# Inverting the first four chunks' triangles by 16 x 16 blocks, with the block products one chunk at a time

## The chip, the cores and the metric

The kernel runs on one core of a Trainium2 chip. Times are device microseconds (us) of one execution. The kernel before took 814.61, 817.60 and 818.12 us in three runs, a median of 817.6 us. One further execution was profiled and took 815.66 us. The engines are named as in the profile: PE (TensorE matmul, with PEld its weight load), DVE (VectorE), ACT (ScalarE), POOL (GpSimd) and SP (SyncE, which here only issues transfers).

## The reference

An attention block with a recurrent state is followed by a feed-forward block. With B = 4 batches, H = 8 heads, S = 768 steps and head size D = 40 the reference computes

```python
for t in range(S):
    y[:, :, t] = einsum('bhd,bhde->bhe', rt, state)
    Sa = einsum('bhde,bhe->bhd', state, at)
    state_decay = state * wt[:, :, None, :] - einsum('bhd,bhe->bhde', Sa, bt)
    state = state_decay + einsum('bhd,bhe->bhde', vt, kt)
x = y.transpose(0, 2, 1, 3).reshape(B * S, H * D)      # 3072 tokens of 320
h = x @ w_in                                           # 320 x 2048
out = (h * cos(h)) @ w_out                             # 2048 x 320
```

All inputs are float32 except that the two weight matrices arrive as float64, seen by the kernel as pairs of 32-bit words.

## The kernel before

**Chunks.** The 768 steps are cut into 24 chunks of C = 32, so that batch x step fills 128 partitions. Within a chunk the recurrence becomes a triangular system of 32 x 32 for each batch and head. Four chunks at a time share one inversion: 4 chunks x 4 batches x 8 heads = 128 triangles, held as the tile `inv` with one triangle part on each partition.

**Preparation of a group of chunks** (`p1_w`, `p1_a`, `p1_b`, `p1_n`): decays `w`, vectors `a` and `b` are loaded, transposed by PE and scaled; `p1_n` multiplies them into the triangles `nps`, which ACT copies to `nt`. `inv_start` (L465) transposes `nt` into `u` on DVE.

**Two ways to invert.** `inverse` (L547) runs `inv_step` (L472) for j = 31 down to 1, each one DVE multiply (L476) and one DVE subtract (L480), then one transpose into `rt` (L484). It serves chunks 0 to 3 and 8 to 23. `by_blocks` (L541) serves chunks 4 to 7 alone. It inverts the two diagonal 16 x 16 blocks together in 15 pairs (`pair_step`, L502 and L507), turns the first block into `rn` (`pair_turn`, L513), and leaves the lower left block to PE: `pair_first` multiplies the raw triangle `noff` by `rn` and ACT copies the product to `half` (L523); `pair_second` multiplies that by the second block and DVE adds the product into `rt` (L535). For this `p1_n` also copies the triangles to `noff` (L455), for chunks 4 to 7 only.

**Work of a chunk c.** `p2_in` and `p2_kn` put v, r and k into padded tiles on POOL; `p2_v`, `p2_k`, `p2_g` transpose them and form two Gram matrices (`gram`, then `ag` and `vvm`). The chain through the state `qz` is `ch_t` (transposes `sT`), `ch_q` (`qps`), `ch_x` (`x0ps`, copied to `x`), `ch_s` (`sps`: `x` times the inverse `rt`, copied to `sm`) and `ch_z` (`dps`; DVE and POOL update `qz` at L721 and L722, and `yt` goes through memory into the token tile `xT`). Chunk 0 starts from a zero state and has no `ch_t` and no `ch_q`.

**The feed-forward block** is cut into pieces: `first_a` and `first_b` (matmuls `ph`, then the cosine on ACT and DVE) and `second` (matmuls `po`). Pieces fill places marked `M` in each chunk's list from chunk 2 on. The weights must be turned into float32 beforehand. `rounded` makes this from 20 tiles of 512 columns: a transfer of `words`, four DVE operations (L241, L242, L251, L257), three on ACT (L245, L247, L254) and one on POOL (L260). These steps wait in the list `w_steps`; `step` takes some after each piece of chunk work (`fill` gives how many).

**Order.** Everything is written out by hand: each engine runs its instructions in the order in which the Python code emits them. `step` also counts down `later` entries, which is how loads and stores get their place in SP's queue. `busy` and `kept_busy` put idle matmuls on PE, `shifted` puts tiny ones. In the built program every transfer from SP waits for the completion of the one eight issues before it. `load` (L146) issues four transfers of 40 KB for one input of one chunk. The tiles `nat_k`, `nat_v` and `nat_r` exist once: their next load waits for POOL to have read them.

**Start of the program** (L953 to L979): preparation of chunks 0 to 3, the decay scan of `w` for chunks 4 to 7 (`scanned(1)`, stored to memory as `wd`), then the 31 inverse steps with the `p2` work of chunks 0 and 1 and `ch_x` of chunk 0 between them.

## Time and profile before

| | before |
|---|---|
| median of three runs | 817.6 us (814.61 to 818.12) |
| profiled execution | 815.66 us |
| its span, first to last instruction | 813.8 us |
| PE busy | 752.8 us, 93% of the span |
| DVE busy | 498.2 us, 61% |
| ACT busy | 385.2 us, 47% |
| POOL busy | 201.3 us, 25% |
| mean granted PE clock | 0.968 of full speed |
| PE busy, 0 to 100 us | 60.2 us |
| PE busy, 100 to 200 us | 93.1 us |
| PE busy, 300 to 700 us | 397.1 us of 400 |

The span is what the engines' records cover; the profiled time has 1.9 us more around it. A group of instructions is shown as line, engine, operation, result <- operands, shapes and count. "Idle before <- X" says what ended the wait ahead of an instruction; "issue" is a wait for nothing that the profile shows. SPq is SP's queue: the time of issuing a transfer, not of moving it. The page cuts the span into 40 slices of 20.3 us, with the busy share in tenths.

### The profile page before, as it was taken

Reading aid. Unit: us, or ns where it says so; the run is one execution under the profiler, and the core shown is the slowest. Engines: PE = TensorE matmul, PEld = TensorE weight load, DVE = VectorE, ACT = ScalarE, POOL = GpSimd, SP = SyncE. Lnnn points to the kernel's source line nnn. Section 1 sums busy time; section 2 is a strip of 40 time slices with the busy share of each in tenths; the row PEclk is TensorE's granted clock in tenths of the full one; section 3 lists DMA queues with packets and bytes.
Section 4 is the critical chain, followed back from the end, with each engine's and each line's share of the span. In section 5 each row is a group of like instructions: output and inputs, shape, how many; then the busy total and the mean of one; then the engine's idle time right before and its main releaser. Section 6 shows DMA issues by size and latency. Waiting matters only on the chain.

```text
span 813.8 us, 38932 instructions
## 1 busy us (share of the span) xinstructions
PE 752.8 (93%) x17472; PEld 579.2 (71%) x17472; DVE 498.2 (61%) x1052; ACT 385.2 (47%) x713; POOL 201.3 (25%) x353
## 2 busy tenths in 40 slices
PE   3647899899899999999999999999999999999997
PEld 3533568677678777777777777777777777777775
DVE  6987888865555797454796554894346773332231
ACT  1214777554255446446436535534635445364352
POOL 5314454430213221231330330331130222201000
PEclk9856899999999999999999999999999999999999
DMA  7366654354144324333214314213220212101000
GB/s 122 59 153 156 188 135 132 52 123 68 44 96 96 62 37 75 69 88 68 62 37 70 100 32 66 60 40 69 50 45 21 45 37 56 24 14 36 19 17 16
DMA packets 183301, 55.74 MB, mean 68 GB/s; under 512 B 157152, under 2 KB 178656, under 8 KB 183136
## 3 DMA queue, kind: packets, MB, share of 16 engines
q1 hardware_dynamic: 180560, 51.95, 29.7%
q8 instruction: 137, 2.24, 1.2%
q10 hardware_dynamic: 2320, 0.98, 0.6%
q0 software_dynamic: 256, 0.33, 0.2%
q14 instruction: 28, 0.23, 0.1%
HBM read 42.07 MB, written 11.14 MB: 65 GB/s over the span
## 4 chain that ended last, share of the span: by engine, by line
PE 67%; DVE 16%; ACT 5%; issue 4%; SPq 4%; DMA 3%; POOL 1%; DVEq 0%; ACTq 0%; POOLq 0%
PE ph L101 22%; PE po L101 20%; SPq L152 4%; PE x0ps L101 4%; PE dps L101 3%; DVE inv_tmp L476 3%; DVE inv L480 3%; PE gram L101 3%; PE vT L326 3%; DVE rw L391 2%; PE sps L101 2%; PE nps L101 2%; PE qps L101 2%; PE sT L623 1%; PE busy L101 1%
## 5 line engine op out<-in xcount | busy, mean ns | idle before, releaser
L101 PE MATMUL po<-w_out_sb,gT 128*128 128x320 f32 x768 | 224.7, 441 | 0.0
L101 PE MATMUL ph<-xT,w_in_sb 128*128 128x256 f32 x768 | 185.3, 386 | 0.6 <-issue 0.6
L101 PEld LDWEIGHTS po<-w_out_sb,gT 128*128 128x128 f32 x768 | 140.8, 191 | 54.7 <-issue 2.5
L101 PEld LDWEIGHTS ph<-xT,w_in_sb 128*128 128x128 f32 x768 | 139.2, 190 | 29.6 <-issue 12.2
L795 ACT ACTIVATE turns<-ph,rnd 128x512 f32<-128x512 f32 x96 | 64.2, 686 | 155.3 <-PE ph L101 154.9
L797 DVE SCALAR_TENSOR_TENSOR turns<-turns,ph 128x512 f32<-128x512 f32 x96 | 64.1, 684 | 116.1 <-ACT turns L795 115.8
L805 DVE TENSOR_TENSOR gT<-ph,turns 128x512 f32<-128x512 f32 x96 | 65.7, 686 | 36.0 <-ACT turns L802 36.0
L722 POOL TENSOR_TENSOR qz<-qz,wc 128x160 f32<-128x160 f32 x92 | 43.0, 486 | 152.1 <-DVE qz L721 151.1
L802 ACT ACTIVATE turns<-turns,half_pi 128x512 f32<-128x512 f32 x96 | 69.3, 722 | 3.1
L801 ACT ACTIVATE turns<-turns 128x512 f32<-128x512 f32 x96 | 60.1, 626 | 18.9 <-DVE turns L797 18.9
L480 DVE TENSOR_TENSOR inv<-inv,inv_tmp 128x31 f32<-128x31 f32 (+15 forms) x155 | 61.9, 399 | 5.3
L476 DVE TENSOR_TENSOR inv_tmp<-u,inv 128x31 f32<-128x31 f32 (+15 forms) x155 | 59.3, 382 | 3.5
L555 POOL COPY vp<-nat_v 128x320 f32<-128x320 f32 x25 | 12.2, 489 | 183.2 <-DMA nat_v<-in_v_dram 113.6
L101 PE MATMUL ph<-xT,w_in_tail 64*128 64x256 f32 x384 | 54.5, 402 | 0.0
L721 DVE TENSOR_TENSOR qz<-dps,qz 128x160 f32<-128x160 f32 x92 | 29.0, 315 | 33.6 <-PE dps L101 33.5
L391 DVE RECIPROCAL rw<-nat_w 128x320 f32<-128x320 f32 x20 | 42.8, 2142 | 0.0
L627 ACT COPY s<-sT 128x512 f32<-128x512 f32 x46 | 24.5, 584 | 37.5 <-PE sT L623 37.5
L101 PEld LDWEIGHTS <-idle 32*64 32x64 bf16 (+2 forms) x566 | 24.7, 95 | 22.2 <-issue 17.1
L101 PEld LDWEIGHTS ph<-xT,w_in_tail 64*128 64x128 f32 x384 | 33.0, 186 | 9.1 <-issue 5.3
L733 POOL TENSOR_TENSOR yt<-yt,wb 128x512 f32<-128x512 f32 x24 | 31.6, 1316 | 22.1 <-DVE yt L728 22.1
L611 ACT COPY vvm<-gram 128x256 f32<-128x256 f32 x24 | 8.8, 367 | 55.4 <-DVE ag L606 55.0
L392 POOL TENSOR_TENSOR bn<-nat_b,rw 128x320 f32<-128x320 f32 x22 | 19.6, 890 | 57.5 <-DVE rw L391 46.1
(131 smaller groups left out, 1106.0 us busy)
## 6 DMA issues: line engine op xcount, KB each, us to landing
words<-in_moe_w_in_dram SPq DMA_DIRECT2D x8, 512.0 KB
nat_k<-in_k_dram SPq DMA_DIRECT2D x96, 40.0 KB
nat_v<-in_v_dram SPq DMA_DIRECT2D x96, 40.0 KB
nat_r<-in_r_dram SPq DMA_DIRECT2D x96, 40.0 KB
xd<-yt SPq DMA_DIRECT2D x48, 80.0 KB
out_dram<-ot SPq DMA_DIRECT2D x24, 160.0 KB
nat_b<-in_b_dram SPq DMA_DIRECT2D x88, 40.0 KB
wd<-ws SPq DMA_DIRECT2D x5, 640.0 KB
```

Source lines behind the costliest of these rows:

```text
L101: nc.tensor.matmul(o, lhsT=lhsT, rhs=rhs, start=start, stop=stop, skip_group_check=True)
L152: via.dma_start(nat[n, c][blk[i], :, :D], at_c.rearrange("h t d -> t h d"))
L391: nc.vector.reciprocal(rw, wn)
L476: nc.vector.tensor_tensor(tmp, u[:, j : j + 1, :j].to_broadcast([P, C - j, j]), x[:, j:, j : j + 1].to_broadcast([P, C - j, j]), ALU.mult,)
L480: nc.vector.tensor_tensor(x[:, j:, :j], x[:, j:, :j], tmp, ALU.subtract)
L722: nc.gpsimd.tensor_tensor(z, z, wc.rearrange("p (f m b) -> p f m b", f=2, m=2)[:, :, :, bb] .unsqueeze(3).to_broadcast([P, 2, 2, D]), ALU. ...
L733: nc.gpsimd.tensor_tensor(yt.rearrange("p j b t -> p (j b) t"), yt.rearrange("p j b t -> p (j b) t"), wx, ALU.mult)
L795: nc.scalar.activation(n, u, ACTF.Identity, bias=rnd, scale=1.0)
L797: nc.vector.scalar_tensor_tensor(n, n, -ROUND, u, ALU.add, ALU.subtract)
L801: nc.scalar.activation(n, n, ACTF.Abs)
L802: nc.scalar.activation(n, n, ACTF.Sin, bias=half_pi, scale=-2.0 * math.pi)
L805: nc.vector.tensor_tensor(gT[:, 2 * e : 2 * e + 2].rearrange("p f t -> p (f t)"), us[e], ns[e], ALU.mult)
```

## The change

`by_blocks` now also makes the inverse of chunks 0 to 3, so `noff` is copied for them too. Their block products are emitted one chunk at a time, ahead of that chunk's `ch_s`: `pair_first(0, 0)` and `pair_second(0, 0)` at the start, F1 and S1 in chunk 1, F2, S2, F3 and S3 in chunk 2. For chunks 0 to 3 `rn` lies in `bn_b[6]` and `half` in `bn_b[4]` and `bn_b[5]`, which are not used for chunks 4 to 6 until later. The products of chunks 4 to 7 become four and four (F4 to F7, S4 to S7) in place of one and three. Loads of `a` and `b` for chunk 4 and `a` for chunk 5 go right behind chunk 0's k, v, r; two weight tiles are fetched next, ahead of chunk 1's k, v, r; `w` of chunks 4 and 5 and `b` of chunk 5 move from the start into chunk 1. The idle matmuls are put in other places and numbers, and `shifted` is 0 at the start where it was 111.

```diff
     bn_b = kept("bn", [P, H, DP], 7, 0.0, padding)
+    for i in (4, 5):
+        nc.gpsimd.memset(bn_b[i][:, :, C // 2 : C], 0.0)
     kn_b = kept("kn", [P, H, DP], 2, 0.0, padding)
...
             G["nt"] = sb1.tile([P, C, 4, 2, HH], F32, tag="nt", name="nt")
-            if c == 4:
+            if c < 8:
                 G["noff"] = sb2.tile([P, 4, 2, HH, C], F32, tag="rt", name="noff")
...
             )
-        if 4 <= c < 8:
+        if c < 8:
             for e in range(2):
...
 
-    def pair_turn():
-        G["rn"] = sb1.tile([P, 4 * H, HB], F32, tag="nt", name="rn")
-        G["half"] = sb1.tile([P, 4 * H, C], F32, tag="u", name="half")
-        nc.gpsimd.memset(G["half"][:, :, HB:], 0.0)
+    def pair_turn(c):
+        if c:
+            G["rn"] = sb1.tile([P, 4 * H, HB], F32, tag="nt", name="rn")
+            G["half"] = sb1.tile([P, 4 * H, C], F32, tag="u", name="half")
+            nc.gpsimd.memset(G["half"][:, :, HB:], 0.0)
+        else:
+            G["rn"] = bn_b[6].rearrange("p h d -> p (h d)").rearrange("p (n u) -> p n u", u=HB)
         nc.vector.transpose(
...
 
-    def pair_first(lo, hi):
-        ps = at("below")[:, 0]
+    def pair_space(c, done, pool, tag):
+        if c or done:
+            return at("below")[:, 0]
+        return pool.tile([P, 512], F32, tag=tag, name="below")
+
+    def pair_half(c, i):
+        return G["half"][:, H * i : H * (i + 1)] if c else bn_b[4 + i % 2][:, :, :C]
+
+    def pair_first(c, i, moe=True):
+        ps = pair_space(c, moe, ps_h, "h")
         nt = G["noff"].rearrange("p c e j t -> p (c e j) t")
-        for n in range(H * lo, H * hi):
+        half = pair_half(c, i)
+        for n in range(H):
             for g in range(B):
-                mm(ps[blk[g], HB * n : HB * (n + 1)], nt[blk[g], n, :], G["rn"][blk[g], n, :], n == H * lo)
-        nc.scalar.copy(
-            G["half"][:, H * lo : H * hi, :HB],
-            ps[:, H * lo * HB : H * hi * HB].rearrange("p (n u) -> p n u", u=HB),
-        )
-
-    def pair_second(c, lo, hi):
-        ps = at("below")[:, 0]
-        rt = G["rts"].rearrange("p c h t -> p (c h) t")
-        for n in range(H * lo, H * hi):
+                mm(
+                    ps[blk[g], HB * n : HB * (n + 1)], nt[blk[g], H * i + n, :],
+                    G["rn"][blk[g], H * i + n, :], n == 0,
+                )
+        nc.scalar.copy(half[:, :, :HB], ps[:, : H * HB].rearrange("p (n u) -> p n u", u=HB))
+        if c + i == 3:
+            nc.gpsimd.memset(padding(bn_b[6]), 0.0)
+
+    def pair_second(c, i, moe=True):
+        ps = pair_space(c, moe, ps_o, "o")
+        half, rt = pair_half(c, i), G["rts"][:, i]
+        for n in range(H):
             for g in range(B):
-                mm(ps[blk[g], HB * n : HB * (n + 1)], G["half"][blk[g], n, :], rt[blk[g], n, HB:], n == H * lo)
-        to = rt[:, H * lo : H * hi, HB:]
+                mm(ps[blk[g], HB * n : HB * (n + 1)], half[blk[g], n, :], rt[blk[g], n, HB:], n == 0)
+        to = rt[:, :, HB:]
         nc.vector.tensor_tensor(
-            to, to, ps[:, H * lo * HB : H * hi * HB].rearrange("p (n u) -> p n u", u=HB), ALU.add
-        )
-        for i in range(lo, hi):
-            G["rt", c + i] = G["rts"][:, i]
+            to, to, ps[:, : H * HB].rearrange("p (n u) -> p n u", u=HB), ALU.add
+        )
+        G["rt", c + i] = rt
 
...
             inv_start, *(lambda j=j: pair_step(j) for j in range(HB - 1, 0, -1)),
-            pair_turn, lambda: inv_end(c, True),
+            lambda: pair_turn(c), lambda: inv_end(c, True),
         ]
...
                     later(1, lambda i=i: load(6 + i, "ab"))
-            elif c >= 2 and c + 3 < NCH:
+            elif c > 4 and c + 3 < NCH:
                 for m in range(6):
-                    later(
-                        8 + m // 3 if c == 2 else (9 if c == 6 else 2) + m, lambda m=m: load(c + 2 + m % 2, "wab"[m // 2])
-                    )
+                    later((9 if c == 6 else 2) + m, lambda m=m: load(c + 2 + m % 2, "wab"[m // 2]))
 
...
         first, other = p1(0), p1(2)
-        for seg in (*first[:2], *other[:2], *first[2:], *other[2:]):
+        for seg in first[:2]:
             step(seg)
+        load(4, "ab")
+        load(5, "a")
+        for seg in (*other[:2], *first[2:], *other[2:]):
+            step(seg)
+        for m in range(2):
+            w_work[m][0]()
         scanned(1)
...
         p2_kn(0)
-        inv_steps.extend(inverse(0))
+        inv_steps.extend(by_blocks(0))
         v, k, g = p2(0)
         v1, k1, g1 = p2(1)
-        for n, seg in ((12, v), (0, k), (0, g), (6, main(0)[2]), (6, None), (4, v1), (0, k1), (0, g1)):
+        x0, s0, z0 = main(0)[2:]
+        for n, seg, idle_n in ((6, v, 0), (0, k, 0), (0, g, 4), (4, x0, 6), (2, v1, 5)):
             for _ in range(n):
                 inv_steps.pop(0)()
-            if seg:
-                step(seg)
-            else:
-                for m in range(3):
-                    w_work[m][0]()
-                p2_in(1)
+            step(seg)
+            if seg is x0:
+                w_work[2][0]()
                 p2_kn(1)
-        N_PAD = {0: 111, 19: 75}
-        shifted(N_PAD[0])
-        while inv_steps:
+            busy(idle_n)
+        while len(inv_steps) > 2:
             inv_steps.pop(0)()
-            if 2 < len(inv_steps) < 9:
-                busy(1, True)
+        step(k1)
+        busy(2)
+        all_of(inv_steps)
+        step(g1)
+        busy(3)
+        N_PAD = {0: 0, 19: 75}
+        step(lambda: pair_first(0, 0, False))
         for m in range(3, 5):
             w_work[m][0]()
+        step(lambda: pair_second(0, 0, False), 0, 1)
+        step(s0, 0, 3)
+        busy(6)
+        step(z0, 0, 4)
+        busy(4)
+        for n, c, name in ((3, 4, "w"), (5, 5, "w"), (7, 5, "b")):
+            later(n, lambda c=c, name=name: load(c, name))
 
...
         M = object()
-        FILL = {(1, 4): 12, (1, 7): 16, (2, 0): 10, (2, 2): 14, (2, 3): 6, (2, 8): 37, (3, 3): 13, (3, 4): 20}
+        firsts = [lambda n=n: pair_first(0, n, n > 2) for n in range(4)]
+        seconds = [lambda n=n: pair_second(0, n, n > 2) for n in range(4)]
+        (F1, F2, F3), (S1, S2, S3) = firsts[1:], seconds[1:]
+        FILL = {(1, 6): 6, (1, 9): 14, (2, 0): 6, (2, 3): 6, (2, 5): 4, (2, 11): 29, (3, 3): 13, (3, 4): 20}
         for c in range(NCH):
...
             q0 = c - c % 4 + 4
-            fill, pn, pn4, blocks = (1, 4), None, None, []
+            fill, pn, pn4 = (1, 4), None, None
             if c == 0:
-                segs = [s, z]
+                segs = []
             elif c == 1:
-                segs = [t, v, q, k, x, g, s, z]
+                segs, fill = [t, F1, v, q, k, S1, x, g, s, z], (1, 4)
             elif c == 2:
-                segs, fill = [t, v, q, k, M, x, M, g, M, s, M, z, M, M], (0, 2)
+                segs, fill = [t, F2, v, q, S2, k, M, x, M, F3, g, M, s, S3, M, z, M, M], (0, 2)
             elif c == 3:
...
                 pw, pa, *p8 = p1(8)
-                F0, F1 = (lambda n=n: pair_first(*n) for n in ((0, 1), (1, 4)))
-                S0, S1 = (lambda n=n: pair_second(4, *n) for n in ((0, 1), (1, 4)))
-                blocks = [F0, S0, F1, S1]
+                firsts = [lambda n=n: pair_first(4, n) for n in range(4)]
+                seconds = [lambda n=n: pair_second(4, n) for n in range(4)]
+                F4, F5, F6, F7 = firsts
+                S4, S5, S6, S7 = seconds
                 segs = [
-                    t, v, M, q, M, k, x, M, F0, M, S0, M, s, M, pw, F1, M, z, M, S1, M, g, M, pa, lambda: scanned(3),
+                    t, v, M, q, M, k, x, M, F4, M, S4, F5, M, s, F6, M, pw, F7, M, z, M, g, M, pa, S5, lambda: scanned(3),
                 ]
...
                 pb, pn = p8
-                segs = [t, M, pb, q, M, pn, k, M, x, M, s, pw, v, M, z, M, g, M, pa, M]
+                segs = [t, M, pb, q, M, pn, k, M, x, M, s, S6, M, pw, v, M, z, S7, M, g, M, pa, M]
             elif c % 4 == 0 and q0 < NCH:
...
                 if seg is not M:
-                    step(seg, *fill, small=seg in (q, x, g, s, z, pn, pn4, *blocks))
-                    if c < 2 or c == 2 and not done:
+                    step(seg, *((0, 0) if c < 3 and seg in (*firsts, *seconds) else fill), small=seg in (q, x, g, s, z, pn, pn4, *firsts, *seconds))
+                    if seg not in (*firsts, *seconds) and (c < 2 or c == 2 and not done):
                         busy({s: 6, q: 5, v: 4, k: 4, z: 4}.get(seg, 3))
```

More of the change, by code (lines that the diff above doesn't have):

```diff
@@ L515, in pair_turn @@
         )
-    def pair_first(lo, hi):
-        ps = at("below")[:, 0]
+    def pair_space(c, done, pool, tag):
[6 more added lines that the diff above has]
+        ps = pair_space(c, moe, ps_h, "h")
         nt = G["noff"].rearrange("p c e j t -> p (c e j) t")
-        for n in range(H * lo, H * hi):
+        half = pair_half(c, i)
+        for n in range(H):
             for g in range(B):
-                mm(ps[blk[g], HB * n : HB * (n + 1)], nt[blk[g], n, :], G["rn"][blk[g], n, :], n == H * lo)
-        nc.scalar.copy(
-            G["half"][:, H * lo : H * hi, :HB],
-            ps[:, H * lo * HB : H * hi * HB].rearrange("p (n u) -> p n u", u=HB),
-        )
-    def pair_second(c, lo, hi):
-        ps = at("below")[:, 0]
-        rt = G["rts"].rearrange("p c h t -> p (c h) t")
-        for n in range(H * lo, H * hi):
-            for g in range(B):
-                mm(ps[blk[g], HB * n : HB * (n + 1)], G["half"][blk[g], n, :], rt[blk[g], n, HB:], n == H * lo)
-        to = rt[:, H * lo : H * hi, HB:]
-        nc.vector.tensor_tensor(
-            to, to, ps[:, H * lo * HB : H * hi * HB].rearrange("p (n u) -> p n u", u=HB), ALU.add
-        )
-        for i in range(lo, hi):
-            G["rt", c + i] = G["rts"][:, i]
+                mm(
[9 more added lines that the diff above has]
+        for n in range(H):
+            for g in range(B):
+                mm(ps[blk[g], HB * n : HB * (n + 1)], half[blk[g], n, :], rt[blk[g], n, HB:], n == 0)
+        to = rt[:, :, HB:]
+        nc.vector.tensor_tensor(
+            to, to, ps[:, : H * HB].rearrange("p (n u) -> p n u", u=HB), ALU.add
+        )
+        G["rt", c + i] = rt
     def by_blocks(c):
```

## The prediction

> **What bounds the kernel now.** I read the page's slices first, then the busy time by stage of work, then the chain through the start, and last the instructions in order of time around the inverse and the block products.
>
> The slices:
>
> ```profile
> PE   3647899899899999999999999999999999999997
> DVE  6987888865555797454796554894346773332231
> PEclk9856899999999999999999999999999999999999
> ```
>
> From the fifth slice on PE is full. Only the first 100 us leave it idle, and there DVE is the full engine. The stages, cut where `sT` of chunks 1 to 5 ends (columns: stretch, its length, then PE, PEld, DVE, ACT and POOL busy with instruction counts, PE clock, DMA share, GB/s):
>
> ```profile
> 30.00:77.00 47.00, 25.30 (x809) 17.30 (x808) 39.20 (x101) 12.58 (x25) 11.55 (x19) 0.62 0.55 127
> 77.00:105.00 28.00, 24.44 (x613) 15.77 (x611) 24.04 (x45) 18.93 (x34) 17.80 (x18) 0.79 0.64 180
> 105.00:138.00 33.00, 31.23 (x678) 24.24 (x677) 27.01 (x48) 25.54 (x44) 15.89 (x17) 1.00 0.47 129
> 180.00:221.00 41.00, 36.43 (x1149) 27.58 (x1147) 21.12 (x53) 15.68 (x30) 6.14 (x13) 0.96 0.32 60
> 221.00:814.00 593.00, 582.29 (x13091) 451.12 (x13091) 332.57 (x723) 282.59 (x525) 117.69 (x212) 1.00 0.25 52
> ```
>
> After 221 us PE is busy 98% of the time. In the built order both kernels have put the same feed-forward matmuls on PE before each later `sT` (24 `ph` before chunk 3's, 72 before chunk 5's), so a front that comes earlier by x us ends the kernel earlier by x us. What sets the front is the chain up to chunk 1:
>
> ```profile
> 50.55 6.83 DMA words<-in_moe_w_in_dram
> ...
> 69.32 2.55 DMA nat_r<-in_r_dram
> ...
> 72.02 0.45 POOL rp L555
> 72.47 1.11 POOL w_in_sb L260
> 73.58 2.95 POOL qz L722 x4
> ```
>
> Two chains end here almost together: SP's issues up to chunk 2's `r`, shown above, and DVE's inverse. The second by its ends:
>
> ```profile
> 34.43 1.25 DVE L468 STREAM_TRANSPOSE u<-nt 128x1024 f32<-128x1024 f32 x1 [0.57 <-ACT nt L449]
> ...
> 62.69 1.91 DVE L484 STREAM_TRANSPOSE rt<-inv 128x1024 f32<-128x1024 f32 x1
> ...
> 64.75 1.25 PE L101 MATMUL sps<-x,rt 32*32 32x72 f32 x64 [1.51 <-DVE rt L484]
> ```
>
> DVE's last product before `qz` ended at 71.65 us, so POOL's `rp` held L260 up by only 0.8 us. An earlier inverse alone would meet the `r` load; the change moves both.
>
> [...] 0.50 granted from 40 to 60 us, where PE is busy 3.3 and 5.3 us of each ten, and 1.00 from 100 us. [...] PE stops inside groups of equal small matmuls with nothing to wait for (2.74 us in `gram` at 90.6 us, 1.99 us in `below`, shown further down). [...] In the trace L241 takes 0.42 us, and 1.38 to 1.49 us where POOL works beside it.
>
> **Part 1, less DVE work.** DVE busy with the two lines of the full inverse, then with the two lines of the block inverse (stretch, length, DVE busy):
>
> ```profile
> 34.00:65.00 31.00, 10.97 (x31) 0.50 0.55 121
> 34.00:65.00 31.00, 11.30 (x31) 0.50 0.55 121
> 176.00:194.00 18.00, 3.81 (x15) 1.00 0.36 64
> 176.00:194.00 18.00, 3.83 (x15) 1.00 0.36 64
> ```
>
> 22.27 - 7.64 = 14.6 us, and 32 gaps of some 0.035 us between instructions = 1.1 us. Added: the `rn` transpose, 1.13 us (seen in chunk 4). ACT's `noff` copies (0.69 us for two) now stand before `bT` and before `vT`, so `u` starts at about 35.1 instead of 34.43. From there: 1.25 + 7.64 + 1.05 (30 gaps) + 1.6 (`ag` and `vvm` of chunk 0, with ACT between) + 0.45 (`x`) + 1.13 + 1.90 + 0.3 = 15.3, so `rt` is there at 50.4 us instead of 64.6. That would be 14.2 us.
>
> **Part 2, what takes its place.** F0 and S0 stand behind chunk 1's `gram` on PE, and ACT's `half` copy behind `vvm` of chunk 1. So `sps` of chunk 0 now waits for chunk 1's `r`. SP: chunk 0's `r` is issued by 26.8; then twelve issues for `a`, `b`, `a` at 0.49 us fill a gap in which SP stood until 31.82 and go on to 32.7; two word tiles to 33.7; `k` and half of `v` to 36.6. The rest of `v` needs the completion of the word tiles (eight issues back). Before, SP was released from words at 57.38 after issuing from 49.58, 7.8 us for 1.57 MB of words and 0.16 MB of `a`: 222 GB/s. Now 1.05 + 0.24 MB take 5.8 us, to 39.0. Two `v` issues and four `r` issues: 42.0; landing +2.55 (as above): 44.5. POOL `rp` 0.68; PE transposes 1.06, five idle matmuls of 0.42 (half clock), `kT` 1.09; ACT 0.59; `gram` 1.6 at half clock: 51.6. DVE `ag` 0.42, ACT `vvm` 0.37: 52.4. PE meanwhile runs three idle matmuls, 1.3, to 52.9; F0 0.9 (0.73 in chunk 4 at full clock), ACT `half` 0.27, S0 0.9, DVE add 0.29: `sps` starts at 55.3, 9.4 us before its old 64.75.
>
> After `sps` (1.25 us, 56.6) the order is close to the old one. One weight step is now issued with S0, so ACT does `expo` and `sign` of tile 0 (1.4 us, behind 0.84 us of DVE) before `sm`: `sm` on DVE ends at 58.3 (was 67.07). Then DVE 0.84 and 0.69; ACT 0.72, 0.66 and 0.72 up to 61.2; the product L257 at 61.9 (was 71.65). POOL: L260 1.15, `qz` 2.95: 66.0 instead of 76.53. POOL no longer waits for chunk 2's `r`: it can be issued after `kn` of chunk 1 (46), so by 52, landing by 55. **Gain at chunk 1's `sT`: 10.5 us.**
>
> **Part 3, chunks 1 and 2.** Added on PE: six groups of 64 at 0.73 us, 1.5 us in chunk 1 and 2.9 in chunk 2. Taken away: 8 and 22 idle matmuls of 0.087 us (37 took 3.23), 0.7 and 1.9. Added on DVE 3 x 0.29, on ACT 3 x 0.27. Twelve more issues on SP in chunk 1 (5.9 us) put weight tiles 7 to 9 some 2 to 3 us later against the front; in the old trace tile 7 is issued at 79.03 and first read at 92.36, 13 us later, so this hides; without that cover it would cost those 2 to 3 us. The POOL memset of `bn_b[6]` waits for F3, but its successors `vp` and `rp` are for chunk 3. PE, DVE and ACT take turns as the limit here, so I charge 0.6 us in chunk 1 and 1.0 in chunk 2. **Cost: 1.6 us.** Chunk 3 is unchanged: nothing.
>
> **Part 4, chunks 4 and 5.** The products are the same 512 matmul records; two more ACT copies and DVE adds (1.1 us less 0.5 saved by the smaller ones) lie under PE's pieces. Before, PE stood still within groups:
>
> ```profile
> 203.94 1.56 PE L101 MATMUL ph<-xT,w_in_sb 128*128 128x256 f32 x6 [0.61 <-issue]
> ...
> 207.67 0.36 PE L101 MATMUL dps<-sm,bn 32*40 32x72 f32 x14 [0.68 <-issue]
> ...
> 213.36 0.91 PE L101 MATMUL below<-rt,half 32*32 32x16 f32 x87 [1.99 <-issue]
> ```
>
> 3.3 us, each behind or in a run of 192 small products. Runs of 64 to 128 should feed better. Bounds: all of it gained (3.3), or the stops only moved (0; no reason for a loss beyond 1). I take half. **Gain: 1.6 us.**
>
> **Sum:** 10.5 - 1.6 + 1.6 = 10.5 us. Against the profiled execution's 815.66 (span 813.8 and 1.9 around it) this gives 805.2; against the median of 817.6 it gives 807.1. I predict 806 us.
>
> **Rivals.**
> - *The loads eat more of it* (15%). If the two word tiles and `k` run at the stretch's mean of 127 GB/s instead of 222, they take 10.2 us and not 5.8; everything to `sps` slips by 4.4 us: 810.5 us. For it: SP waits for words in the old chain. Against it: the queue is otherwise empty at 33 us.
> - *More is gained* (13%). The 2.74 us stop in `gram` and all 3.3 us of chunk 4 vanish, and PE gets its full clock before chunk 1: 10.5 + 2.7 + 1.7 + 1 = 801 us (nearer 800 by the profile's own time). For it: other idle matmuls keep PE busier from 39 us on. Against it: `gram` keeps its 128 records.
> - *The front is earlier and is given back* (5%): if the weight chain (DVE, ACT, words) rather than the recurrence sets chunk 2's first pieces, PE waits at `ph` for about what was gained: 815 us. Against it: the weight tiles move forward too, tiles 3 and 4 by about 18 us (from 69.87 to 52).
> - *Slower, the clock* (7%). Chunks 1 and 2 hold 56 us of PE work. [...] Each us of full-clock work then costs one more: from the forecast's 806 it decides at 11.6 us of such work (817.6), and 18 us of it, a third of those two chunks, give 824. Against it: chunk 2 holds pieces of 1.9 us that themselves keep PE busy.
> - My own forecast has 60%.
>
> **How the numbers follow.** About 0.5% (4.1 us) is what a measurement of this kernel tells from no change. The forecast's own range is 802 to 810.5. Faster than 813.5: 60 + 13 + 11 of the loads' 15 = 84%. Within 0.5%: the loads' other 4 (with the word tiles still slower) and the 5 of the gain given back = 9%. Slower: 7%. The range of eight in ten has to take in the loads' case at 810.5 with 2 us beyond and the better case at 801: 800 to 812.5.
>
> **What would show it.** Right: `rt` by the block inverse at about 50 us, `sps` of chunk 0 at 54 to 57, chunk 1's `sT` done near 66, chunk 3's at 128 to 130 (138.1 before), `below` without a stop of 1 us. Wrong: `sps` of chunk 0 behind a wait for `nat_r` or `nat_v` later than 46 us; PEclk below 0.9 in chunk 2; a stretch from chunk 1's to chunk 3's `sT` longer than 64 us (61 before); new waits at `sps` of chunks 4 to 7 for DVE's add.

## The result and the profile after

Over 20 runs of each the changed kernel takes 813.15 us in the median (807.84 to 820.08), the kernel before 816.61 us (813.42 to 820.40). The ratio is 0.9959, 95% interval 0.9943 to 0.9976: 3.4 us faster, where 10.5 were forecast. The time lies above the range of the prediction and within the 0.5% that count as no change. The changed kernel's runs scatter more than the old one's.

The profiled execution took 814.53 us (span 812.8), only 1.1 us less than that of the kernel before. Its slices, the same three rows of the page as in the prediction:

```profile
PE   3678799799999999999999999999999999999997
DVE  6948858855743797553895554994346873332231
PEclk9878699999999999999999999999999999999999
```

DVE is relieved in the third slice (4 tenths for 8) and the sixth (5 for 8). PE's clock is better in the third and fourth (0.7 and 0.8 for 0.5 and 0.6) and lower in the fifth (0.6 for 0.8). The stretches between the ends of `sT` of chunks 1 to 5 (columns as in the prediction):

```profile
30.00:68.80 38.80, 28.85 (x819) 18.11 (x819) 23.32 (x63) 10.19 (x22) 8.31 (x15) 0.74 0.61 153
68.80:101.50 32.70, 25.03 (x728) 16.11 (x726) 29.27 (x52) 22.45 (x40) 19.97 (x20) 0.80 0.62 162
101.50:135.60 34.10, 33.01 (x918) 25.49 (x916) 23.33 (x48) 24.37 (x43) 13.03 (x16) 0.99 0.43 116
135.60:181.20 45.60, 40.50 (x958) 31.84 (x956) 32.77 (x58) 25.27 (x48) 17.83 (x29) 0.96 0.40 94
181.20:217.20 36.00, 33.77 (x1022) 26.44 (x1022) 22.68 (x53) 15.41 (x31) 6.17 (x13) 1.00 0.30 55
```

Chunk 1's `sT` ends 8.4 us earlier (68.8 against 77.3). But chunk 1 then takes 32.7 us instead of 27.7, chunk 2 34.1 instead of 33.1 and chunk 3 45.6 instead of 42.7, so at 181.2 nothing is left (180.8 before). Chunk 4 is 5.2 us shorter, chunks 5 and 6 are 1.4 and 1.6 us longer. (A chunk is measured here from the end of its `sT` to the end of the next one's.)

The DVE chain of the start, in order of time:

```profile
46.20 1.07 DVE L518 STREAM_TRANSPOSE bn<-inv 128x512 f32<-128x512 f32 x1
47.16 1.93 DVE L486 STREAM_TRANSPOSE rt<-inv 128x1024 f32<-128x1024 f32 x1
52.70 0.42 DVE L621 TENSOR_TENSOR ag<-gram,su 128x256 f32<-128x256 f32 x1 [3.61 <-PE gram L101]
```

`rt` is there at 49.1 us (50.4 forecast); then DVE waits for chunk 1's `gram`. PE's side of the same place, and POOL's `rp`:

```profile
55.12 0.42 PE L101 MATMUL below<-bn,noff 32*32 32x16 f32 x27 [1.28 <-issue]
...
58.67 0.72 PE L101 MATMUL sps<-x,rt 32*32 32x72 f32 x28 [0.99 <-issue]
...
64.72 1.00 PE L101 MATMUL dps<-sm,bn 32*40 32x72 f32 x42 [0.82 <-issue]
```

```profile
46.62 0.45 POOL L570 COPY rp<-nat_r 128x320 f32<-128x320 f32 x1 [1.80 <-DMA nat_r<-in_r_dram]
```

Chunk 1's `r` lands 2.1 us later than worked out (46.6 against 44.5), and PE stops three times inside groups of equal matmuls, 3.1 us together. A stop is idle time ahead of an instruction that waits for nothing the profile shows ("issue"). And this is what PE does ahead of chunk 2's `sT`:

```profile
94.01 0.86 PE L101 MATMUL dps<-sm,bn 32*40 32x72 f32 x62
94.80 1.04 PE L101 MATMUL busy<-idle 128*128 128x512 bf16 x4
98.81 1.01 PE L101 MATMUL spare<-idle 128*128 128x192 bf16 x6 [2.97 <-issue]
99.61 1.92 PE L638 MATMUL sT<-ident,qz 128*128 128x128 f32 x8
```

POOL's last `qz` of chunk 1 ended at 97.7. The six idle matmuls behind the stop hold up `sT` for two us more. Counted from the start of the program, PE's stops in this stretch come after 466, 721, 848, 976, 1358, 1486 and 1742 matmul records (a float32 product counts as two: the 32 products of one F or S group are 64 records of `below`): always a multiple of some 127.4 apart. That gave three theories: (1) PE's instructions come in blocks, and a block comes late where the one before is used up quickly; (2) chunk 1's `r`, now behind two weight tiles, holds the front; (3) DVE, ACT and POOL hold it with the weight steps and the added products.

### The profile page after: what moved, and what is told of

It is laid out like the page before. It is cut to its first block, busy times and chain, and to the rows that moved or that the text cites. A ratio compares the mean times of both kernels' runs of the same rounds, so it can differ in the third digit from the quotient of the medians.

```text
span 812.8 us, 39682 instructions
## 1 busy us (share of the span) xinstructions
PE 758.7 (93%) x17859; PEld 582.0 (72%) x17859; DVE 485.8 (60%) x1025; ACT 387.1 (48%) x723; POOL 199.4 (25%) x354
## 4 chain that ended last, share of the span: by engine, by line
PE 68%; DVE 15%; DMA 4%; issue 4%; ACT 4%; SPq 3%; POOL 1%; DVEq 0%; ACTq 0%; POOLq 0%
PE ph L101 23%; PE po L101 19%; PE x0ps L101 4%; PE dps L101 3%; DVE inv_tmp L478 3%; SPq L152 3%; PE gram L101 3%; DVE inv L482 3%; PE vT L328 2%; DVE rw L393 2%; PE sps L101 2%; PE busy L101 2%; PE nps L101 2%; PE qps L101 2%; PE sT L638 1%
## 5 line engine op out<-in xcount | busy, mean ns | idle before, releaser
L482 DVE TENSOR_TENSOR inv<-inv,inv_tmp 128x31 f32<-128x31 f32 (+15 forms) x124 | 51.2, 413 | 4.3
L478 DVE TENSOR_TENSOR inv_tmp<-u,inv 128x31 f32<-128x31 f32 (+15 forms) x124 | 48.5, 391 | 2.3
L101 PEld LDWEIGHTS <-idle 32*64 32x64 bf16 (+2 forms) x443 | 21.5, 101 | 24.3 <-issue 19.7
L702 DVE TENSOR_TENSOR sm<-sps,su 128x128 f32<-128x128 f32 x48 | 11.7, 285 | 34.1 <-ACT sm L697 31.3
```

The source lines that it names most:

```text
L101: nc.tensor.matmul(o, lhsT=lhsT, rhs=rhs, start=start, stop=stop, skip_group_check=True)
L478: nc.vector.tensor_tensor(tmp, u[:, j : j + 1, :j].to_broadcast([P, C - j, j]), x[:, j:, j : j + 1].to_broadcast([P, C - j, j]), ALU.mult,)
L482: nc.vector.tensor_tensor(x[:, j:, :j], x[:, j:, :j], tmp, ALU.subtract)
```

## The experiments

Single profiles of one and the same start differ by over 3 us at chunk 1's `sT`, so what follows uses medians of runs where it can, and for places within the program the traces of all kernels that share the start.

**Part 4 alone, and all but Part 4.** On the kernel before, the lists of chunks 4 and 5 as in the changed one:

```diff
-    F0, F1 = (lambda n=n: pair_first(*n) for n in ((0, 1), (1, 4)))
-    S0, S1 = (lambda n=n: pair_second(4, *n) for n in ((0, 1), (1, 4)))
+    F4, F5, F6, F7 = (lambda n=n: pair_first(n, n + 1) for n in range(4))
+    S4, S5, S6, S7 = (lambda n=n: pair_second(4, n, n + 1) for n in range(4))
```

> The kernel before, with only Part 4 of the change: the block products of chunks 4 to 7 divided chunk by chunk (F4 to F7, S4 to S7 at the places of the changed kernel); the start is as before. Theory A (what is left of the gain is Part 4's, the front's is lost again before chunk 3): some 3 us faster than before, 813.5, with chunk 4 five us shorter (41.2 to 36) and chunk 5 one to two longer. Theory B (Part 4 only moves the stops inside groups): within 1 us of before, 816.

And on the changed kernel the old division:

```diff
-    t, v, M, q, M, k, x, M, F4, M, S4, F5, M, s, F6, M, pw, F7, M, z, M, g, M, pa, S5, lambda: scanned(3),
+    t, v, M, q, M, k, x, M, F4, M, S4, M, s, M, pw, F57, M, z, M, S57, M, g, M, pa, lambda: scanned(3),
```

> The changed kernel with Part 4 taken back: the products of chunks 4 to 7 are one and three again, at their old places; the new start stays. Theory A (the front's gain is gone by chunk 3): about 816, no better than before. Theory B (the front still gives 2 to 3 us at chunk 3's sT and keeps them): 813 to 814, and chunk 3's sT at 135 to 136 as in the changed kernel (138.1 before).

The division alone: 813.05 us, ratio 0.9967 (0.9951 to 0.9984). The new start alone: 815.1 us, 0.9986 (0.9972 to 1.0). Theory A comes nearer: what is left of the gain is mostly Part 4's, 2.2 to 2.8 us. The start seems to add about one, but its interval reaches to no gain. Chunk 4 took 35.8 us with the division on the old start (41.2 before) and 44.9 without it on the new one, where PE stood still for 5.2 us within groups.

**Is it the place in the block?**

```diff
                 p2_kn(1)
+                shifted(64)
             busy(idle_n)
```

> The changed kernel with 64 tiny matmuls on PE behind x of chunk 0, where PE waits for chunk 1's r, so that every later instruction of PE stands half a block of 128 matmul records further on. Theory 1 (the stops inside groups are instruction blocks that come late): the stops keep their record counts (721, 848, 976, 1358, 1486, 1742), so they fall 64 records earlier in the work, in other groups, and chunk 3's sT moves by 1 to 4 us either way. Theories 2 (the loads) and 3 (the engines): the stops stay with their groups (F0, sps, dps, x0ps) or go nowhere, and the time stays within 0.5 us of the changed kernel, since PE has nothing to do at that place.

828.62 us, 15 us slower, which no forecast had, for 64 tiny matmuls that run while PE has nothing to do. The stops keep their counts, so they now fall 64 records earlier in the work, as PE's timeline shows:

```profile
82.99 0.32 PE L101 MATMUL gram<-aT,kT 40*32 40x32 f32 x25 [1.65 <-issue]
86.45 0.48 PE L101 MATMUL sps<-x,rt 32*32 32x72 f32 x32 [1.30 <-issue]
116.47 0.36 PE L101 MATMUL gram<-rT,vT 40*32 40x32 f32 x15 [2.60 <-issue]
169.85 2.93 PE L101 MATMUL po<-w_out_sb,gT 128*128 128x320 f32 x7 [2.88 <-issue]
178.48 0.33 PE L101 MATMUL nps<-aT,bT 40*32 40x32 f32 x24 [1.79 <-issue]
```

They left F0, `dps` and the idle matmuls ahead of `sT`, and chunk 2's `sT` started at 96.4, 3.2 us earlier than in the changed kernel. But other stops came into chunk 3 (4.7 us) and, up to 2 us each, into later chunks as far as 19 and 22, and with them most of the 15 us. One stop cost more than its length: behind the one of 2.0 us in chunk 19 PE's clock was 0.84 from 657 to 668 us, and eight `po` took 3.6 us, for 2.3 ahead of it. Theories 2 and 3 had no room for stops that move with the count.

**The disputed cost by itself.** 255 products like those of `below` at three places:

```diff
+        def dense(n):
+            ps = at("dense")
+            for i in range(n):
+                mm(ps[blk[i % B], 0, :HB], ident[blk[i % B], blk[i % B]], ident[blk[i % B], :HB], True)
...
                 p2_kn(1)
+                dense(255)
...
+            if c in (2, 21):
+                dense(255)
```

> The changed kernel with the disputed cost by itself: 255 products of 32x32 by 32x16 (510 matmul records, four blocks of some 127) put on PE at three places: behind x of chunk 0 (some 40 us, where k, v, r and the word tiles are loaded), ahead of chunk 2 (some 105 us, words still loading), and ahead of chunk 21 (some 690 us, where only chunk inputs and stores move). Each is 5.8 us of work at 11.4 ns a record, what 64 of below take (0.73 us), and 8 to 12 us at half clock. Theory 1 (blocks come late): the group stands still three or four times inside, each stop about 127 records behind the last; a block takes 3.4 to 5.7 us in the first two places, 14 to 20 us for the group, and less in the quiet one, under 10 us. Theory 3 (engines; no fetch): no stop inside any of the three, 5.8 to 6.5 us each at full clock.

856.57 us in its one run. PE's timeline, the three groups:

```profile
39.20 0.77 PE L101 MATMUL dense<-ident 32*32 32x16 f32 x66
42.12 1.91 PE L101 MATMUL dense<-ident 32*32 32x16 f32 x128 [2.16 <-issue]
45.85 1.91 PE L101 MATMUL dense<-ident 32*32 32x16 f32 x128 [1.82 <-issue]
50.40 1.90 PE L101 MATMUL dense<-ident 32*32 32x16 f32 x128 [2.65 <-issue]
54.41 1.04 PE L101 MATMUL dense<-ident 32*32 32x16 f32 x60 [2.10 <-issue]
...
112.77 1.90 PE L101 MATMUL dense<-ident 32*32 32x16 f32 x128 [2.48 <-issue]
117.04 1.90 PE L101 MATMUL dense<-ident 32*32 32x16 f32 x128 [2.38 <-issue]
...
714.67 1.25 PE L101 MATMUL dense<-ident 32*32 32x16 f32 x128 [1.21 <-issue]
718.14 1.90 PE L101 MATMUL dense<-ident 32*32 32x16 f32 x128 [2.22 <-issue]
```

128 records run in 1.25 to 1.9 us, and ahead of the next PE stands still for 1.2 to 2.7 us, waiting for nothing that the profile shows. From one restart to the next it takes 3.7 to 4.6 us in the first two places and, behind the block of 1.25 us, 3.47 in the quiet one. So in a row of such blocks each cost at least 3.5 us, and 0.3 to 1.1 us more in the first two places, where more is transferred (94 to 142 GB/s in the page's slices there, 60 in that of the quiet place); that the quiet place would take under 10 us was wrong (11.2). The page has a queue of the kind `instruction` whose packets follow the number of PE's instructions, one row of the DMA queues for the changed kernel, then for this one:

```profile
q8 instruction: 140, 2.29, 1.2%
```

```profile
q8 instruction: 152, 2.49, 1.2%
```

140 packets of 16 KB; PE has 17,859 matmuls and as many weight loads, and 35,718 / 140 = 255 instructions a packet. The 1,530 records more of this kernel (3,060 instructions) brought 12 packets. In the changed kernel's trace packets of this queue start at 52.9, 56.3, 62.1, 79.8, 83.6 and 96.4 us, and PE starts again at 55.12, 58.67, 64.72, 82.50, 86.23 and 98.81: 2.2 to 2.7 us later each time. Behind three others, at 68.2, 72.0 and 87.7, no stop shows.

**Fewer transfers.** In each of the two kernels, from tile 5 on:

```diff
+                if m >= 5:
+                    cols, part = slice(cols.start, cols.start + 64), part[:, :64]
```

> The changed kernel with an eighth of the weight transfer from tile 5 on: each transfer of words brings 64 of its columns, and the conversion reads these eight times over, so every instruction stays and the feed-forward weights are not the true ones; left out is the transfer of seven eighths of 15 weight tiles, 6.9 MB between 55 and 180 us. Theory 1 (instruction blocks come late because the transfers are in their way): the stops inside groups in chunks 0 and 1 fall from 8.3 us to under 3, chunk 2's sT comes 4 to 5 us earlier, and the kernel takes 807 to 809. Theory 2 (chunk 1's r is late behind word tiles 0 and 1, which stay whole) and theory 3 (DVE, ACT and POOL set the front): chunk 2's sT moves by less than 1 us, the stops stay, and the time is 812 to 813.

> The kernel before with an eighth of the weight transfer from tile 5 on, as in the run of the changed kernel with few words: all instructions stay, the feed-forward weights are not the true ones; left out are seven eighths of the transfer of 15 weight tiles. Theory 1 (the words hold up the changed kernel's instruction blocks more than the old one's): the old kernel gains 0 to 1.5 us, 814.5 to 816.5, less than the 2.8 us that the changed one gained, and its stops in chunk 1 fall from 3.4 to about 2. Rival (the words are late for their own sake, or hold up other loads, in both kernels alike): it gains 2.8 us or more, 813 or less.

The changed kernel takes 810.35 us (ratio to before 0.9935, 0.9918 to 0.9952, for 0.9959 with whole tiles: 2.0 us less, 2.8 by the medians), the old one gains nothing (817.93; 1.0007, 0.9992 to 1.0021). The stop ahead of chunk 2's `sT` shrinks to 0.96 us and the one in `x0ps` to 0.83, so chunk 2's `sT` starts at 96.0. F0, `sps` and `dps` of chunk 0 keep their stops; tiles 0 to 4 still come whole there. Theory 1's sign is right for the changed kernel, its size is not: the stops of chunks 0 and 1 fell from 8.3 to 7.1 us and not to under 3, and those of the old kernel's chunk 1 stayed at 3.5. So the transfers are a part of why a block is late, and not the main one.

**Chunk 1's r first.**

```diff
-        for m in range(2):
-            w_work[m][0]()
         scanned(1)
...
             step(seg)
+            if seg is v:
+                for m in range(2):
+                    w_work[m][0]()
```

> The changed kernel with weight tiles 0 and 1 fetched behind chunk 1's k, v and r instead of ahead of them. Theory 2 (chunk 1's r, late behind these two tiles, holds the front): POOL's rp of chunk 1 is freed near 43 instead of 46.6, gram of chunk 1 and everything behind it come 3 us earlier, chunk 1's sT starts at 62 to 64 (65.3 to 67.3 in the two runs of that order so far), and the kernel takes 810. Theory 1 (late instruction blocks) and theory 3 (engines: DVE, ACT and POOL still have the weight steps ahead of qz): rp comes earlier too, but chunk 1's sT by less than 1 us, because PE's stops or the weight steps take it up; 812.5 to 814.

813.45 us (0.9948, 0.9926 to 0.9969): of theory 2's 3 us no more than 0.9 shows, within the noise. In the profiled execution, which at 820.55 us was the longest of its fifteen and so counts for less, PE's transposes of `r` come 2.1 us earlier (45.0 against 47.1), but F0's stop is 3.4 us, `dps` has 2.2, and chunk 1's `sT` ends at 68.9, as in the changed kernel. The median and the trace both speak against theory 2.

**Without the products of chunks 0 to 3.**

```diff
         ps = pair_space(c, moe, ps_h, "h")
+        if not c:
+            return
...
+        if not c:
+            G["rt", i] = G["rts"][:, i]
+            return
```

> The changed kernel without F0 to F3 and S0 to S3, so the lower left block of the inverses of chunks 0 to 3 stays zero and the output is not the reference's; left out are 512 records on PE (four instruction blocks, so later ones keep their place to within 3 records), four copies on ACT and four adds on DVE. Theory 3 (what the products cost is their own work): chunk 1's stretch shortens by F1 and S1 alone, 1.5 us, chunk 2's by 2.2 to 2.9, and chunk 3's sT comes some 4 to 6 us earlier, of it 1 to 2 before chunk 1's sT; about 808. Theory 1 (each group of small matmuls also brings a block that comes late): the stops of chunks 0 and 1 fall from 8 to 11 us to about 5 besides, chunk 1's stretch is 29 instead of 32 to 34, and the kernel takes 804 to 806.

810.33 us (0.9927, 0.9899 to 0.9954). Neither forecast was right. 512 records less save some 2.7 us, not more: chunk 1 is as long as with them (32.8 us from `sT` to `sT`), because stops stay: 4.0 us in `dps` of chunk 0, 2.5 ahead of chunk 2's `sT`. And up to DVE's first `qz` of chunk 1 nothing moves relative to chunk 1's `sT` (25.6 us, 26.1 with the products). What sets that distance is DVE's weight work. From the end of `sT` to the first `qz` DVE is busy for all but 3.4 to 4.0 us, 20.7 us before and 22.7 after (stretch, length, DVE busy, clock, DMA share, GB/s):

```profile
77.27:101.92 24.65, 20.69 (x33) 0.77 0.66 186
```

```profile
68.83:94.91 26.08, 22.65 (x39) 0.80 0.64 158
```

And these are its products alone (L257 before, L259 after), of before, after and the kernel without F and S:

```profile
77.27:101.92 24.65, 5.46 (x7) 0.77 0.66 186
```

```profile
68.83:94.91 26.08, 5.73 (x8) 0.80 0.64 158
```

```profile
68.26:93.87 25.61, 5.74 (x8) 0.90 0.68 160
```

Eight weight products instead of seven. In both kernels DVE does eight from chunk 0's first `qz` to chunk 1's, in the same order. Before, it did the first of them while POOL's `rp` and L260 held up POOL's part of `qz`, and with it `sT`; with that wait gone the tile falls behind `sT`, into chunk 1. Theory 3 has this part of the loss.

**Where the time goes.** The mean times of kernels with the new start (the changed one, the one with Part 4 undone, two runs with S7 later, one with another list in chunk 5) against those with the old start (before, the division alone, two with other lists in chunk 5):

| | old start (4 traces) | new start (5) | gain |
|---|---|---|---|
| chunk 1's `sT` ends | 76.4 | 68.5 | 7.9 |
| DVE's first `qz` of chunk 1 | 101.0 | 94.9 | 6.1 |
| chunk 2's `sT` ends | 104.3 | 102.4 | 1.9 |
| chunk 3's `sT` ends | 137.2 | 136.8 | 0.4 |
| chunk 4's `sT` ends | 179.8 | 180.5 | -0.7 |

Among traces of one start the ends of `sT` differ by 2.6 to 4.7 us, so the last two gains are not clear of nothing; most of the steps from one line to the next scatter less. The largest step, 4.2 us, lies between DVE's first `qz` and the end of `sT`: 3.1 to 3.6 us in each of the four traces with the old start, 6.6 to 8.3 in the five with the new. In each of the latter the idle matmuls ahead of `sT` have the stop, 2.97 to 4.53 us.

**That one boundary moved.** First a try that takes 59 idle matmuls of chunks 1 and 2 out and as many tiny ones in at the start, which moves the boundaries between these places:

```diff
+                shifted(59)
...
-        FILL = {(1, 6): 6, (1, 9): 14, (2, 0): 6, (2, 3): 6, (2, 5): 4, (2, 11): 29, (3, 3): 13, (3, 4): 20}
+        FILL = {(1, 6): 6, (3, 3): 13, (3, 4): 20}
```

> The changed kernel with 59 idle matmuls taken out of chunks 1 and 2 (14, 6, 6, 4 and 29 of them, each about 0.087 us) and 59 tiny ones put behind x of chunk 0, where PE waits for chunk 1's r: from chunk 2's end on every instruction has its old place in its block, in between each stands up to 59 records later. Theory 1 (place in the block decides): chunk 2's sT starts at 96 to 97 as with the 64 tiny matmuls (99.6 without), chunk 3 has no stop of over 1 us (4.7 us with the 64), and the kernel takes 807 to 810. Against it (the idle matmuls are there for PE's clock, or fill waits that stay): the waits for sm, qz and ACT in chunks 1 and 2 grow by what is taken out, or the granted clock falls below 0.9, and the time is 812 to 816.

815.22 us (0.9984, 0.9963 to 1.0005): theory 1's 807 to 810 was wrong, and the rival's 812 to 816 came. With 14 idle ones gone ahead of `dps` the boundary was only 45 records from its old place and fell into `dps` itself, a stop of 4.0 us, and chunk 2 then waited 3.4 us for DVE's `gT`. This run alone does not decide between the two. Then without taking anything out of chunk 1:

```diff
+                shifted(64)
...
-        FILL = {..., (2, 5): 4, (2, 11): 29, (3, 3): 13, (3, 4): 20}
+        FILL = {..., (2, 5): 4, (3, 3): 13, (3, 4): 20}
...
+                if (c, i) == (2, 11):
+                    kept_tiny(92)
```

> The changed kernel with 64 tiny matmuls behind x of chunk 0 (PE waits there anyway) and, ahead of chunk 2's S3, 92 tiny ones in the place of 29 idle ones of the same length (2.5 us): from there on every instruction has its old place in its block (64 - 29 + 92 = 127 records, one block), and up to there each stands half a block further. Theory 1, sharpened (one block that begins inside dps of chunk 1 comes late right ahead of chunk 2's sT): from DVE's first qz of chunk 1 to that sT it takes 1.6 to 2.4 us (4.7 to 6.4 in five runs of the old placing), chunk 3's sT starts at 132 to 133.5 (134.6 to 137.2 before), chunk 3 has no stop of 1 us or more, and the kernel takes 810 to 811.5. Rival (the time lost there would come back as waits of PE for DVE's weight steps in chunk 2): chunk 3's sT at 134.5 or later, and 813.

810.63 us (0.9935, 0.9920 to 0.9951). PE's timeline around `dps` of chunk 1:

```profile
85.35 0.48 PE L101 MATMUL sps<-x,rt 32*32 32x72 f32 x32 [1.57 <-issue]
...
90.76 0.43 PE L101 MATMUL dps<-idle 32*64 32x288 bf16 x4 [2.13 <-DVE sm L702]
...
94.50 0.66 PE L101 MATMUL spare<-idle 128*128 128x192 bf16 x6
95.00 1.04 PE L638 MATMUL sT<-ident,qz 128*128 128x128 f32 x8
```

The boundary now lies in `sps`. The next packet of `q8` starts at 86.4 us. By the 2.2 to 2.7 us of the changed kernel I estimate its first matmul at 88.6 to 89.1, where PE waits for `sm` anyway (from 88.6 to 90.8), and `sT` starts 1.9 us after DVE's first `qz` (4.7 in the changed kernel). Chunk 3's `sT` starts at 132.0, chunk 3 has no stop of over 0.3 us, and the forecast of theory 1 is met in each number. Chunk 2 gives some of it back: from the start of its `sT` to the next it takes 37.0 us, with a stop of 2.7 in `gram` (35.0 in the changed kernel). The edit moves every boundary from the start to chunk 2's S3 by half a block, not this one alone.

**S7.** The trace of the changed kernel shows S7 waiting for the PSUM tile that `dps` holds, and chunk 6's first piece for its tokens:

```profile
242.87 0.72 PE L101 MATMUL below<-rt,half 32*32 32x16 f32 x64 [1.44 <-DVE yt L743]
...
252.73 1.99 PE L101 MATMUL ph<-xT,w_in_sb 128*128 128x256 f32 x8 [1.48 <-DMA xT<-xd]
```

```diff
-    segs = [t, M, pb, q, M, pn, k, M, x, M, s, S6, M, pw, v, M, z, S7, M, g, M, pa, M]
+    segs = [t, M, pb, q, M, pn, k, M, x, M, s, S6, M, pw, v, M, z, M, S7, g, M, pa, M]
```

> The changed kernel with S7 one feed-forward piece later in chunk 5, so that it no longer stands directly behind dps, whose PSUM tile it takes over. Theory X (S7's wait of 1.44 us for DVE's yt is lost time): the wait goes and the kernel is 1.2 to 1.4 us faster, 811.8. Theory Y (the way of chunk 5's tokens through memory sets when chunk 6's ph can start): PE reaches that ph earlier and waits there 2.9 us instead of 1.5; no gain, 813.

> The changed kernel with S7 one piece later, a second time, beside the others on one chip: 811 to 812 if the 811.4 of the first run stands, 813 if that run was a lucky one.

811.38 us (0.9925, 0.9898 to 0.9953), and 809.66 the second time (0.9922, 0.9905 to 0.9939). Chunk 5 is 1.5 us shorter, and the wait of chunk 6 has not grown:

```profile
243.17 0.73 PE L101 MATMUL below<-rt,half 32*32 32x16 f32 x64
...
250.51 1.99 PE L101 MATMUL ph<-xT,w_in_sb 128*128 128x256 f32 x8 [1.27 <-DMA xT<-xd]
```

Theory X holds. By the second series, whose interval lies apart from the changed kernel's, this version beats both kernels. Two more lists, `z` one piece earlier besides, on the new and on the old start, and S7 alone on the old start:

```diff
-    ..., x, M, s, S6, M, pw, v, M, z, S7, M, g, M, pa, M]
+    ..., x, M, s, S6, pw, v, M, z, M, S7, g, M, pa, M]
```

> The changed kernel with chunk 5's list changed: no feed-forward piece between S6 and the next chunk's w, so z stands one piece (2.4 us) earlier ahead of chunk 6's ph, and S7 behind the piece that follows z. Theory X (the token tile's way through memory, begun at z, makes the 1.3 to 1.5 us wait of chunk 6's ph): that wait goes as well as S7's, and the time is 810 to 811, 2.5 to 3 us under the changed kernel. Theory Y (another input sets chunk 6, such as the padded b from POOL, which bT waited for in other runs): a wait of 0.9 to 1.4 us stays in chunk 6, and only S7's is saved: 811.5.

> The kernel before, its start with the full inverse untouched, with the products of chunks 4 to 7 divided and chunk 5's list as in the run before this one. If the new start is worth nothing by the time chunk 4 begins (theory 1), this comes within 1.5 us of that run, 810 to 812. If it is worth the 2 to 3 us that some traces show at chunk 3's sT, it is 2 to 3 us slower, 813 to 814.

> The kernel before with its old start, the products of chunks 4 to 7 divided, and S7 one piece later. If the new start is worth nothing once its late block is counted, this is as fast as the changed kernel with S7 later, 811 to 812.5, and slower than the kernel with the moved blocks by 1.5 to 3 us. If the new start is worth 2 us, it is 813.5.

With `z` earlier: 814.11 us on the new start (0.9966, 0.9947 to 0.9985; 810 to 811 were expected) and 812.57 on the old (0.9948, 0.9933 to 0.9964). The wait of chunk 6 does go on the new start (29.0 us from `sT` to `sT`), but a stop of 0.9 in `dps` and a wait of 0.7 for `rt` come to chunk 5. S7 alone on the old start: 811.52 (0.9951, 0.9935 to 0.9967). In four pairs that differ in the start alone the new one is 0.7, 1.1 and 2.4 us faster and 1.5 us slower. The mean is 0.7 us, which four values that spread so far do not tell from nothing.

Last, both repairs together, the moved boundary and S7 one piece later:

> The kernel of the run before this one with S7 one feed-forward piece later in chunk 5 as well. If the two gains lie at different places they add: 1.4 to 1.8 us under that run, 808.5 to 810. If chunk 6's ph waits longer for its tokens instead (2.5 us or more), nothing.

810.63 us (0.9941, 0.9918 to 0.9965). In the profile chunk 5 is 1.5 us shorter than with the moved boundary alone, but the median is the same, and no better than S7 later alone (809.66): 808.5 to 810 were expected, and the gains do not add as far as these runs tell.

## Why the prediction was wrong

**Part 1 was right.** `rt` was there at 49.1 us, for 50.4 forecast.

**Part 2 was right in kind, 2.6 us too large.** Chunk 1's `r` was read at 46.6 instead of 44.5 and `sps` of chunk 0 began at 57.0 instead of 55.3; with the stops in F0, `sps` and `dps` chunk 1's `sT` ended at 68.5 in the mean (66.0 forecast). The late `r` is hardly what cost it: where `r` came 2.1 us earlier, the stops were longer instead.

**Part 3 failed.** It charged 0.6 us for chunk 1, 1.0 for chunk 2 and nothing for chunk 3, from the busy time of the added and removed matmuls. By the table the gain shrinks by 6.0 us in chunk 1, 1.5 in chunk 2 and 1.1 in chunk 3. The prediction's own sign of this came: 66.8 us from chunk 1's `sT` to chunk 3's. The parts:
- 1.8 us because DVE does a weight tile more between `sT` and `qz`. The sum of Part 2 counted POOL's wait in the old start as lost time; DVE had used it. At chunk 0's first `qz` on DVE the new start is 5.0 us ahead in the same traces (65.6 for 70.6), at chunk 1's 6.1: for DVE the 7.9 us at `sT` were never there. This is read from the traces; no run takes that tile away alone. This is the third rival's chain, at another place than that rival put it.
- 4.2 us by one block boundary ahead of chunk 2's `sT`. In each run in which the boundary fell elsewhere (`shifted(64)`, and the two with the moved boundary) `sT` started 1.2 to 2.1 us after `qz`, for 4.7 to 6.4; of these 4.2 us the kernel's time kept 2.0 by the ratios, and none where S7 stood later as well. The step that failed here is the sentence that the stop in `gram` stays because it "keeps its 128 records". With `shifted(64)` the stops kept their counts and left their groups: they belong to the count of records before them, not to the group. The prediction saw the stops and still priced none of them: it moved the boundaries by some hundred records and did not ask where they would fall.
- 1.5 us in chunk 2, 0.5 more than charged. Chunk 2 is full on PE and has F2, F3, S2 and S3; its mean clock was 0.97 to 0.99 in the new traces and 1.00 in the old.
- 1.1 us in chunk 3, where the lists are the same. All of it is in two of the five new traces (45.6 and 44.9 us; 42.1 to 43.0 in the others, 42.3 to 42.9 in the old). There PE's clock falls after its wait for `nat_a`, as in the changed kernel's profile (0.57 from 160 to 164 us) and not in that with S7 later (1.00 there):

```profile
160.02 0.72 PE L328 MATMUL aps<-ident,nat_a 128*128 128x128 f32 x4 [1.57 <-DMA nat_a<-in_a_dram]
160.53 3.53 PE L101 MATMUL ph<-xT,w_in_sb 128*128 128x256 f32 x8
```

```profile
162.37 0.63 PE L328 MATMUL aps<-ident,nat_a 128*128 128x128 f32 x4 [1.24 <-DMA nat_a<-in_a_dram]
162.84 1.89 PE L101 MATMUL ph<-xT,w_in_sb 128*128 128x256 f32 x8
```

Over all traces of this case the same eight `ph` were slow behind six of the eight waits of 1.33 to 1.60 us and behind none of the shorter ones. Why the clock falls behind one such wait and not behind another was not tried and stays open, and so does whether the new start makes this wait longer.

**Part 4 was right, and somewhat more.** Forecast 1.6 us, bounds 0 to 3.3; measured 2.2 to 2.8, and some 4 with S7 moved. The stops within chunk 4 did go (3.3 to 0.5 us). Not foreseen: S7 waits 1.44 us directly behind `z`. The prediction looked for a new wait at `sps`, not at the PSUM tile.

**The sum.** 7.9 at chunk 1's `sT`, 8.6 lost by chunk 4's (for 1.6 charged), 2.2 to 2.8 in chunks 4 to 6: some 2 us from the traces; the medians give 3.4. Among the rivals "the loads eat more of it" had chunk 1's `r` late (2.1 us of its 4.4), but fetching `r` first brought nothing that shows. "The front is earlier and is given back", held at 5%, came nearest in its number, and in part by luck: the changed kernel's PE does not wait at `ph` in chunk 2, and DVE's weight work has 1.8 of the 8.6 us. "More is gained" was right that the stop in `gram` could go, but others came in its place. "Slower, the clock" did not come: PE's clock was 0.80 in chunk 1 (0.79 before) and 0.99 in chunk 2 (1.00), and 0.84 from 90 to 100 us, where it had been 0.66 around the stop in `gram`.

## What to carry to other kernels

Where an engine runs long rows of small matmuls, count instructions as well as time: find the stops "on issue" inside equal groups, see whether they are a fixed count apart, and ask where an edit moves the next ones, above all those that follow a dense group and precede a link of the critical chain. In the run with the moved boundary the packet behind it came about where PE waited 2.13 us for `sm` anyway, and `sT` started 1.9 us after `qz`, for 4.7: a few tiny instructions in an idle place had put it there, and others made the count good again later. And before a wait is booked as gain, look at what the engine behind it did in that time.

## What was not expected of the hardware

In each of four pages the queue `q8 instruction` has one packet of 16 KB for every 255 of PE's matmuls and weight loads, that is for some 128 matmuls: 34,944 to 137 packets before, 35,718 to 140 in the changed kernel, 34,694 to 136 without F and S of chunks 0 to 3, 38,778 to 152 with the dense groups. In the quiet place of the dense groups packets start at 711.9, 715.7 and 719.2 us, and PE starts again at 714.67 and 718.14. So there the next packet starts 1.1 us after PE has begun the block before, and its first matmul runs 2.4 to 2.7 us after that (2.2 to 2.7 in the changed kernel). A row of such blocks took no less than 3.47 us each, 27 ns a matmul, at 60 GB/s, and 3.7 to 4.6 us at 94 to 142. `below` runs at 11 ns a record (64 in 0.73 us) and `dps` at some 13 (62 in 0.86 us), and PE has stopped for up to 4.5 us at a boundary behind such a group. A single dense block behind slowly used ones passed without a stop (128 records of `gram` in 1.3 us at 646 us of the changed kernel, behind eight `po` of 2.3 us).
